# The low part of a converted weight group is subtracted one step later, and the conversions begin one step later in the first slot

## The chip, the cores and the metric

The kernel runs on one core of one Trainium2 chip. The metric is the device time of one execution in microseconds (us); lower is better. Time before: a median of 1327.45 us over three executions (1324.56 to 1330.62).

## What is computed

Linear attention over 8 x 8 heads of 576 tokens, then a mixture of eight experts of which each token takes one, then a feed-forward network with a leaky ReLU:

```python
h = np.maximum(x[mask] @ w1[e], 0.0)
out[mask] = gate_w[mask, None] * (h @ w2[e])      # 4608 tokens, 512 -> 1024 -> 512
...
h = x @ w_in                                       # 512 -> 2048
g = np.maximum(0.01 * h, h)
return g @ w_out                                   # 2048 -> 512
```

The weights `w_in` and `w_out` arrive as float64 words; the kernel turns them into float32 itself, by integer operations on their halves.

## The kernel before

Products of float32 are formed from halves: `split` (L508) lets ScalarE round a tile to a high part (L509, a CAST) and VectorE subtract it from the source, which leaves the low part (L510). TensorE then adds three products: high by high, low by high, high by low.

The experts' work is cut into slots of 512 tokens of one expert. Nine slots are always run (the first of them, slot 0, is in two functions, `slot0` and `slot0b`), and the rest stand under branches. A slot has two passes. In **pass 1** (`pass1`, L657) eight groups of 12 matmuls (L666) make the hidden rows; each group is followed by a ReLU on ScalarE (L668), which writes the high part, and by its low part on VectorE (L669). In **pass 2** (`pass2`, L672) four groups of 24 matmuls (L677) make the output rows; each is copied out by ScalarE (L683) and stored.

Beside them a slot prepares the next one, in an order that is written out by hand, every engine doing its instructions in that order:

- `wsplit` splits a quarter of an expert's weights, staged in a ring of five tiles `st` (L600): four for this slot's second product during pass 1, four for the next slot's first product during pass 2.
- `xload` gathers the next slot's tokens by GpSimd (L632), `xgate` scales the four gathered tiles on ScalarE (L641).
- `xprep(k)` turns a quarter of them by four transposes on TensorE into one of **two** buffers `tp` in PSUM (L652); ScalarE writes the high part (L654), VectorE the low part (L655), which frees the buffer. In slots 1 to 8 quarters 0 and 1 are turned in the middle of pass 2's second group, quarters 2 and 3 in the middle of its third; in `slot0b` in the middle of the third and the fourth.

Into slots 0 to 7 the conversion of `w_in` and `w_out` is woven. `conversions` is a generator: its first step loads the first of 16 groups into a tile `w` (L708, two DMAs of 512 KB, from ScalarE's queue; later groups are loaded from SP's), then each group takes four steps in `f64`. Step 1: two operations on VectorE (L724, L725), then `behind()`, the stores of the group before (L741, L742), and `ahead()`, the load of the next group. Step 2: L729, L730. Step 3: L732, L733. Step 4: four short operations (L737, `r`), the high part `rh` by ScalarE and the low part `rl` by VectorE.

`slot(s)` calls a step after pass 1's groups 1, 3, 5 and 7 (from slot 4 on also after group 6), after pass 2's groups 0, 1 and 2, and in the middle of group 3. `slot0b` calls five steps: after groups 0, 1 and 2, in the middle of group 3 and after it. So in slots 1, 2, 3 and 7 a group's step 4 falls after pass 1's last group, and step 1 of the next one after pass 2's group 0.

Of the kernel before, what the change touches and what calls it, by code (L numbers as in the profile page):

```python
# [9 lines left out]
F32 = mybir.dt.float32  # L10
# [4 lines left out]
ALU = mybir.AluOpType  # L15
# [492 lines left out]
def split(nc, hi, lo, src, eng=None):  # L508
    nc.scalar.copy(out=hi, in_=src)  # L509
    (eng or nc.vector).tensor_tensor(out=lo, in0=src, in1=hi.bitcast(F32), op=ALU.subtract)  # L510
# [33 lines left out]
def experts(pools, tc, cst, a, region, xd, dense, did, wops):  # L544
    nc = tc.nc
# [60 lines left out]
    def loads_to(n):  # L606
        while nload[0] < min(n, len(items)):
            wload(*items[nload[0]])
            nload[0] += 1

    def wsplit(s, which, c, eng=None, most=len(items)):
        n = 8 * s + 4 * (which - 1) + c
        loads_to(n + 1)
        t = stage.pop((s, which, c))
        if which == 1:
            split(nc, w1h[:, :, 256 * c:256 * c + 256], w1l[:, :, 256 * c:256 * c + 256], t.rearrange("p (k f) -> p k f", k=4), eng)
        else:
            split(nc, w2h[:, 2 * c:2 * c + 2], w2l[:, 2 * c:2 * c + 2], t.rearrange("p (k f) -> p k f", k=2), eng)
        loads_to(min(n + 1 + AHEAD, most))

    def idload(s):
        if s < NSLOT:
            nc.sync.dma_start(out=idts[s % 3].rearrange("p t c -> p (t c)"),
                              in_=region[bass.ds(reg(s, 1, NE * NT), SLOT), :].rearrange("(p t) c -> p (t c)", t=4))
# [11 lines left out]
    def xload(s):  # L636
        xids(s)
        xgather(s)
# [4 lines left out]
    def xgate(s):  # L643
        for t in range(4):
            xgate1(s, t)
# [3 lines left out]
    def xprep(k, wait=False):  # L649
        tp = ps2.tile([128, 4, 128], F32, tag="t", name="tp")  # L650
        for t in range(4):
            nc.tensor.transpose(out=tp[:, t], in_=xg[:, t, 128 * k:128 * k + 128], identity=ident)  # L652
        hi, lo = (x[:, k].rearrange("d (p t) -> d t p", t=4) for x in (xh, xl))
        nc.scalar.copy(out=hi, in_=tp)  # L654
        low = lambda: nc.vector.tensor_tensor(out=lo, in0=tp, in1=hi.bitcast(F32), op=ALU.subtract)  # L655
        if wait:
            xlow[k] = low  # L657
        else:
            low()
# [12 lines left out]
    def pass2(d, o, mid, rows):  # L672
        yp = ps.tile([128, SLOT], F32, tag="kv", name="yp")
        n = 0
        for f in range(8):
            for w, h in ((w2h, hh[:, f]), (w2l, hh[:, f]), (w2h, hl[f])):
                nc.tensor.matmul(yp[:, rows], lhsT=w[:, f, 128 * d:128 * d + 128], rhs=h[:, rows], start=(n == 0), stop=(n == 23))  # L677
                n += 1
            if f == 3:
                mid()  # L680
        y = ys[cnt[1] % 2]
        cnt[1] += 1
        nc.scalar.copy(out=y[:, rows], in_=yp[:, rows])  # L683
        nc.scalar.dma_start(out=dense[128 * d:128 * d + 128, bass.ds(o, rows.stop)], in_=y[:, rows])
# [26 lines left out]
    def f64(cv, name, i, w, ahead, behind):  # L711

        V = nc.vector
        if name == "win":
            dst = wops["win"][i % 4].rearrange("p s h k f -> h k p s f")[:, i // 4]
        else:
            dst = wops["wout"].rearrange("s p h k f -> h k p s f")[:, i]
        w2 = w.rearrange("p b f w -> p (b f) w")
        lo, hi = w2[:, :, 0], w2[:, :, 1]
        r = cv.tile([128, 8, 256], F32, tag="r", name="r")  # L720
        rh = cv.tile([128, 7, 256], F32R, tag="rh", name="rh")
        rl = cv.tile([128, 7, 256], F32R, tag="rl", name="rl")
        t = r[:, 0:4].rearrange("p b f -> p (b f)").bitcast(I32)
        V.tensor_scalar(out=t, in0=hi, scalar1=0x7FFFFFFF, scalar2=None, op0=ALU.bitwise_and)  # L724
        V.tensor_scalar(out=t.bitcast(F32), in0=t.bitcast(F32), scalar1=CLAMP_LO, scalar2=CLAMP_HI, op0=ALU.max, op1=ALU.min)  # L725
        behind()
        ahead()
        yield
        V.tensor_scalar(out=lo, in0=lo, scalar1=29, scalar2=0x40000000, op0=ALU.logical_shift_right, op1=ALU.bitwise_xor)  # L729
        V.tensor_scalar(out=t, in0=t, scalar1=4, scalar2=1, op0=ALU.logical_shift_left, op1=ALU.logical_shift_right)  # L730
        yield
        V.tensor_tensor(out=t, in0=t, in1=lo, op=ALU.bitwise_xor)  # L732
        V.scalar_tensor_tensor(out=t, in0=hi, scalar=-0x80000000, in1=t, op0=ALU.bitwise_and, op1=ALU.bitwise_or)  # L733
        yield
        for k, (x, y, op) in enumerate(((0, 2, ALU.add), (4, 1, ALU.subtract), (1, 0, ALU.subtract), (3, 5, ALU.subtract)) if name == "win"
                                       else ((0, 1, ALU.subtract), (2, 4, ALU.subtract), (2, 0, ALU.subtract), (3, 5, ALU.subtract))):
            V.tensor_tensor(out=r[:, 4 + k], in0=r[:, x], in1=r[:, y], op=op)  # L737
        split(nc, rh, rl, r[:, 1:8])

        def store():  # L740
            nc.sync.dma_start(out=dst[0], in_=rh.bitcast(F32))  # L741
            nc.sync.dma_start(out=dst[1], in_=rl.bitcast(F32))  # L742

        yield store

    def conversions(cv):
        todo = [(name, i) for name in ("win", "wout") for i in range(8)]
        w = {0: f64_load(cv, *todo[0], nc.scalar)}
        yield

        def ahead(n):
            if n < len(todo):
                w[n] = f64_load(cv, *todo[n])

        store = lambda: None
        for n, (name, i) in enumerate(todo):
            for r in f64(cv, name, i, w.pop(n), lambda: ahead(n + 1), store):
                store = r or store
                yield
        store()  # L760
# [33 lines left out]
    def slot0b(step):  # L794
        rows = slice(0, SLOT)
        xload(1)
        loads_to(8 + AHEAD)
        idload(2)
        for t in range(4):
            def mid():  # L800
                if t == 0:
                    wsplit(1, 1, 0)
                elif t == 1:
                    xgate(1)
                else:
                    xprep(2 * t - 4)
                    xprep(2 * t - 3)
                if t == 3:
                    step()
            pass2(t, 0, mid, rows)  # L810
            if t < 3:
                wsplit(1, 1, t + 1)
            step()

    def slot(s, step=lambda: None, mid2=lambda t: None, rows=slice(0, SLOT), end=NSLOT):
        if s + 1 < NSLOT:
# [33 lines left out]
    def rest(ctx, pre):  # L850
        wp = ctx.enter_context(tc.tile_pool(name="wp", bufs=1, reuse_waits="tile"))
        ys.extend(wp.tile([128, DM], F32, name=f"y{i}") for i in range(2))
        with ExitStack() as cctx:
            conv = conversions(cctx.enter_context(tc.tile_pool(name="cv", bufs=1, side="right", reuse_waits="tile")))
            step = lambda: next(conv, None)
            slot0b(step)
            for s in range(1, NSTATIC - 1):
                slot(s, step=step)
            for _ in conv:
                pass  # L860
# [455 lines left out]
```

## Time and profile before

| | |
|---|---|
| median of the runs | 1327.45 us (1324.56 to 1330.62) |
| the profiled execution's own time | 1331.54 us |
| its span, first to last instruction | 1329.7 us |
| TensorE busy | 1284.1 us, 97% |
| VectorE busy | 1044.5 us, 79% |
| ScalarE busy | 601.8 us, 45% |
| GpSimd busy | 348.3 us, 26% |
| mean granted TensorE clock | 0.991 |
| DMA | 274.69 MB, mean 207 GB/s |

The profile shows one execution. 1.9 us of its time lie outside the span. A share over the whole span says little here, since the program has four stages (attention to about 163 us, the experts' slots to 606 us, then the two products of the feed-forward network). What a change in the slots is worth is read there: from how long a slot's two passes take, and from what TensorE waits for.

### The profile page before, as it was taken

How to read it: one execution, taken by the hardware profiler on the slowest of the kernel's cores; microseconds unless marked ns; L12 is line 12 of the kernel's file. 1: busy time of each engine (PE TensorE's matmuls, PEld its weight loads, DVE VectorE, ACT ScalarE, POOL GpSimd, SP SyncE). 2: the span in 40 equal slices, each digit the busy share in tenths (PEclk: the TensorE clock that was granted, in tenths of full speed). 3: DMA queues.
4: the chain of work that ended last, by engine and by line, in shares of the span. 5: the costliest groups of instructions: out<-in, count | busy, mean ns of one | idle time of the engine just before them, and what ended most of it. 6: DMA issues, size and time to landing. Idle time of an engine off the chain costs nothing.

```text
span 1329.7 us, 21460 instructions
## 1 busy us (share of the span) xinstructions
PE 1284.1 (97%) x8161; PEld 1159.2 (87%) x8161; DVE 1044.5 (79%) x1375; ACT 601.8 (45%) x956; POOL 348.3 (26%) x283
## 2 busy tenths in 40 slices
PE   6999799999999999999999999999999999999998
PEld 6888677888888877899999999999978888888887
DVE  5789866788778878655888888888788888888886
ACT  4656435554555556452333233333244444444543
POOL 2227851011101110111433434433412221121121
PEclk9999899999999999999999999999999999999999
DMA  9876437879789887867833343333895354443430
GB/s 370 349 282 206 145 108 249 271 248 307 252 276 294 289 272 236 280 205 262 318 119 128 128 158 128 131 124 126 340 369 187 119 158 143 136 150 121 128 119 32
DMA packets 143088, 274.69 MB, mean 207 GB/s; under 512 B 17920, under 2 KB 67584, under 8 KB 142080
## 3 DMA queue, kind: packets, MB, share of 16 engines
q1 hardware_dynamic: 117936, 203.73, 45.5%
q10 hardware_dynamic: 17488, 48.48, 9.1%
q0 software_dynamic: 7552, 21.02, 4.5%
q8 instruction: 66, 1.08, 0.3%
q14 instruction: 46, 0.38, 0.1%
HBM read 176.87 MB, written 96.32 MB: 205 GB/s over the span
## 4 chain that ended last, share of the span: by engine, by line
PE 52%; issue 24%; POOL 6%; DMA 3%; DVE 3%; ACT 1%; another core or an unknown queue 1%; POOLq 0%; ACTq 0%; SPq 0%; DVEq 0%
PE hp L971 25%; PE hp L666 13%; PE yp L677 13%; POOL out L1156 4%; DMA wi<-wid 1%; PE tp L652 1%; DMA xg<-xd,idi 1%; POOL region L363 1%; DMA hd<-ht 1%; POOL q L227 0%; DVE xv L510 0%; POOL xg L632 0%; DVE xq L655 0%; ACT rh L509 0%
## 5 line engine op out<-in xcount | busy, mean ns | idle before, releaser
L971 PE MATMUL hp<-xh,wi 128*128 128x256 f32 x1152 | 211.4, 281 | 1.0 <-DMA wi<-wid 0.8
L666 PE MATMUL hp<-xq,xk 128*128 128x512 f32 (+1 forms) x640 | 189.7, 380 | 0.3 <-DVE xr L262 0.3
L971 PEld LDWEIGHTS hp<-xh,wi 128*128 128x128 f32 x1152 | 179.6, 189 | 1.3 <-ACT xh L509 1.0
L971 PE MATMUL hp<-x,wi 128*128 128x256 f32 x1296 | 161.5, 283 | 1.9 <-issue 1.8
L971 PE MATMUL hp<-xl,wi 128*128 128x256 f32 x576 | 161.8, 281 | 0.0
L971 PEld LDWEIGHTS hp<-x,wi 128*128 128x128 f32 x1296 | 157.9, 190 | 2.2 <-issue 2.2
L632 POOL DMA_INDIRECT xg<-xd,idi x44 | 54.8, 1245 | 356.4 <-ACT xq L668 228.1
L677 PE MATMUL yp<-xq,xk 128*128 128x512 f32 (+1 forms) x400 | 142.1, 385 | 0.8 <-DVE xq L669 0.8
L666 PEld LDWEIGHTS hp<-xq,xk 128*128 128x128 f32 x640 | 118.4, 189 | 23.3 <-DVE xr L262 0.8
L1156 POOL DMA_INDIRECT out<-yo,cf x36 | 59.3, 1647 | 291.7 <-DVE yo L1153 289.3
L1171 PE MATMUL yp<-wi,x 128*128 128x256 f32 x480 | 134.5, 280 | 1.2 <-DVE x L510 1.0
L1170 PE MATMUL yp<-wi,wi 128*128 128x512 f32 x384 | 134.8, 392 | 0.5 <-ACT wi L509 0.5
L510 DVE TENSOR_TENSOR xv<-st,xk 128x1024 fp32r<-128x1024 f32 x77 | 94.6, 1230 | 48.0 <-ACT xk L509 46.8
L677 PE MATMUL yp<-xq,xv 128*128 128x512 f32 (+1 forms) x320 | 122.0, 381 | 0.0
L666 PE MATMUL hp<-xq,xv 128*128 128x512 f32 (+1 forms) x320 | 121.3, 379 | 0.0
L985 DVE SCALAR_TENSOR_TENSOR ht<-ht 128x1024 f32<-128x1024 f32 (+1 forms) x73 | 112.5, 1550 | 1.9
L971 PEld LDWEIGHTS hp<-xl,wi 128*128 128x128 f32 x576 | 108.7, 189 | 0.0
L1018 POOL TENSOR_TENSOR s<-s,s 128x512 f32<-128x512 f32 x36 | 49.5, 1375 | 181.6 <-DVE s L1015 99.7
L1171 PEld LDWEIGHTS yp<-wi,x 128*128 128x128 f32 x480 | 90.1, 188 | 2.1 <-DVE x L510 2.1
L509 ACT CAST xk<-st 128x1024 fp32r<-128x1024 f32 x80 | 83.5, 1046 | 14.8 <-ACT y L683 8.3
L677 PEld LDWEIGHTS yp<-xq,xk 128*128 128x128 f32 x400 | 75.2, 190 | 14.9 <-DVE xq L669 1.2
L1170 PEld LDWEIGHTS yp<-wi,wi 128*128 128x128 f32 x384 | 72.1, 188 | 16.6 <-ACT wi L509 0.8
(227 smaller groups left out, 2804.9 us busy)
## 6 DMA issues: line engine op xcount, KB each, us to landing
st<-in_w SPq DMA_DIRECT2D x80, 512.0 KB
hd<-ht ACTq DMA_DIRECT2D x70, 512.0 KB
xt<-hd SPq DMA_DIRECT2D x18, 1024.0 KB
wi<-hd SPq DMA_DIRECT2D x18, 1024.0 KB
wi<-wid SPq DMA_DIRECT2D x28, 512.0 KB
v<-in_v SPq DMA_DIRECT2D x16, 650.0 KB
wi<-wod SPq DMA_DIRECT2D x5, 2048.0 KB
k<-in_k SPq DMA_DIRECT2D x16, 576.0 KB
```

The lines of the kernel that those rows point to most:

```text
L363: ins = nc.gpsimd.indirect_dma_start(out=region, out_offset=bass.IndirectOffsetOnAxis(ap=t["ix"][:, c:c + 1], axis=0), in_=t["tg"][:, c], ...
L509: nc.scalar.copy(out=hi, in_=src)
L510: (eng or nc.vector).tensor_tensor(out=lo, in0=src, in1=hi.bitcast(F32), op=ALU.subtract)
L632: nc.gpsimd.indirect_dma_start(out=xg[:, t], out_offset=None, in_=xd[0:n], in_offset=bass.IndirectOffsetOnAxis(ap=idis[s % 2][:, t:t + 1], ...
L666: nc.tensor.matmul(hp[:, rows], lhsT=w[:, k, 128 * f:128 * f + 128], rhs=x[:, k, rows], start=(n == 0), stop=(n == 11))
L677: nc.tensor.matmul(yp[:, rows], lhsT=w[:, f, 128 * d:128 * d + 128], rhs=h[:, rows], start=(n == 0), stop=(n == 23))
L971: self.nc.tensor.matmul(bank[:, g], lhsT=w[:, h, k, 128 * g:128 * g + 128], rhs=x[:, k], start=(n == 0), stop=(n == 5))
L985: V.scalar_tensor_tensor(out=c, in0=c, scalar=0.01, in1=c, op0=ALU.mult, op1=ALU.max)
L1018: G.tensor_tensor(out=s[6], in0=s[6], in1=s[5], op=ALU.add)
L1156: ins = nc.gpsimd.indirect_dma_start(out=out, out_offset=bass.IndirectOffsetOnAxis(ap=idi[s % 2][:, t:t + 1], axis=0), in_=yo[s % 2][:, t] ...
L1170: nc.tensor.matmul(bank, lhsT=oh[:, k], rhs=w[i][:, :, k], start=(fresh and k == 0), stop=False, skip_group_check=not fresh)
L1171: nc.tensor.matmul(bank[:, 1], lhsT=ol[:, k], rhs=w[i][:, 0, k], start=False, stop=(k == 7), skip_group_check=not fresh)
```

## The change

Four edits, in two parts.

The low part: `rl` is no longer computed in step 4, right behind ScalarE's cast to `rh`, but in the store function, just before the two stores are issued. `behind()`, which runs that function for the group before, moves from the end of step 1 to its start, ahead of L724 (L725 in the new numbering).

The steps of `slot0b`: none is taken after group 0; two, one behind the other, are taken after group 3. So the first load of the conversions and every step of the first group come one place later; from slot 1 on the steps lie as before.

```diff
         lo, hi = w2[:, :, 0], w2[:, :, 1]
+        behind()
         r = cv.tile([128, 8, 256], F32, tag="r", name="r")
...
         V.tensor_scalar(out=t.bitcast(F32), in0=t.bitcast(F32), scalar1=CLAMP_LO, scalar2=CLAMP_HI, op0=ALU.max, op1=ALU.min)
-        behind()
         ahead()
         yield
...
-        split(nc, rh, rl, r[:, 1:8])
+        nc.scalar.copy(out=rh, in_=r[:, 1:8])
 
         def store():
+            V.tensor_tensor(out=rl, in0=r[:, 1:8], in1=rh.bitcast(F32), op=ALU.subtract)
             nc.sync.dma_start(out=dst[0], in_=rh.bitcast(F32))
             nc.sync.dma_start(out=dst[1], in_=rl.bitcast(F32))
...
             pass2(t, 0, mid, rows)
             if t < 3:
                 wsplit(1, 1, t + 1)
-            step()
+            if t:
+                step()
+            if t == 3:
+                step()
```

VectorE's order from the last step of a group in slot 1 (after pass 1) to the two low parts of the gathered tokens in the middle of pass 2's second group; `xv` is the low part of a quarter of weights, `xq<-tp` that of a quarter of tokens:

```order
 L737 TENSOR_TENSOR r<-r 128x256 x4
-L510 TENSOR_TENSOR rl<-r,rh 128x1792
 L510 TENSOR_TENSOR xv<-st_110,xk 128x4x256
 L510 TENSOR_TENSOR xv<-st_111,xk 128x4x256
-L724 TENSOR_SCALAR r<-w 128x1024
-L725 TENSOR_SCALAR r<-r 128x1024
+L741 TENSOR_TENSOR rl<-r,rh 128x1792
+L725 TENSOR_SCALAR r<-w 128x1024
+L726 TENSOR_SCALAR r<-r 128x1024
 L655 TENSOR_TENSOR xq<-tp,xq 128x4x128 x2
```

The long subtraction goes from the far side of two weight splits to the near side: it now stands between them and the tokens' low parts, which free the `tp` buffers.

ScalarE's order in `slot0b`, from the copy of pass 2's group 0 to the casts of the first turned tokens, before:

```order
L683 COPY y_2208<-yp 128x512
L684 DMA dense<-y_2208 128x512
L509 CAST xk<-st_113 128x4x256
L708 DMA w<-in_win 128x2x512 x2
L641 ACTIVATE xg<-xg,idt_115 128x512 x4
L683 COPY y_2209<-yp 128x512
L684 DMA dense<-y_2209 128x512
L509 CAST xk<-st_109 128x4x256
L654 CAST xq<-tp 128x4x128 x2
```

And in the change, the same place:

```order
L683 COPY y_2208<-yp 128x512
L684 DMA dense<-y_2208 128x512
L509 CAST xk<-st_113 128x4x256
L641 ACTIVATE xg<-xg,idt_115 128x512 x4
L683 COPY y_2209<-yp 128x512
L684 DMA dense<-y_2209 128x512
L509 CAST xk<-st_109 128x4x256
L708 DMA w<-in_win 128x2x512 x2
L654 CAST xq<-tp 128x4x128 x2
```

The load of the first group goes from ahead of the four scalings of the gathered tokens to behind them. The load of the second group, on SP's queue, moves behind one more load of the ring (`st_109`) in the same way.

## Rows read from the trace of the kernel before

**Rows 1.** The page's part 1: busy us, share of the span, instructions of each engine.

```profile
PE 1284.1 (97%) x8161; PEld 1159.2 (87%) x8161; DVE 1044.5 (79%) x1375; ACT 601.8 (45%) x956; POOL 348.3 (26%) x283
```

**Rows 2.** Windows over pass 2 of slots 0 to 7: length, busy by engine, PEclk, DMA.

```profile
187.55:216.58 29.03, 25.85 (x113) 20.82 (x112) 14.06 (x18) 13.38 (x17) 5.12 (x4) 0.94 0.85 298
238.34:261.91 23.57, 23.57 (x113) 19.68 (x112) 17.57 (x21) 14.47 (x17) 0.00 (x0) 1.00 0.76 235
283.67:307.25 23.58, 23.58 (x114) 19.68 (x112) 17.57 (x21) 14.50 (x17) 0.00 (x0) 1.00 0.70 213
329.01:352.58 23.57, 23.57 (x113) 19.68 (x112) 17.56 (x21) 14.51 (x17) 0.00 (x0) 1.00 0.71 210
374.34:399.02 24.68, 23.87 (x113) 19.60 (x112) 19.37 (x25) 14.94 (x18) 0.00 (x0) 1.00 0.74 243
420.78:444.41 23.63, 23.63 (x114) 19.66 (x112) 20.55 (x23) 15.02 (x18) 0.00 (x0) 1.00 0.91 294
466.17:491.13 24.96, 24.01 (x114) 19.58 (x112) 20.79 (x25) 14.49 (x17) 0.00 (x0) 1.00 0.95 296
512.89:538.04 25.15, 24.30 (x113) 19.59 (x112) 19.82 (x23) 14.43 (x17) 0.00 (x0) 1.00 0.65 214
```

**Rows 3.** Groups by line and form: busy us, mean ns, idle before and releaser.

```profile
L510 DVE TENSOR_TENSOR rl<-r,rh 128x1792 fp32r<-128x1792 f32 x16 | 32.4, 2026 | 28.4 <-ACT rh L509 28.4
L509 ACT CAST rh<-r 128x1792 fp32r<-128x1792 f32 x16 | 27.2, 1698 | 53.1 <-DVE r L737 50.8 <-DMA idt<-region 2.3
```

**Rows 4.** Timeline of ScalarE and its queue in slot0b: start, us, instruction.

```profile
194.28 2.17 ACTq L708 DMA_DIRECT2D w<-in_win  x2
...
204.49 0.72 ACT L641 ACTIVATE xg<-xg,idt 128x512 f32<-128x512 f32 x1 [0.65 <-DMA xg<-xd,idi]
```

**Rows 5.** Timeline of TensorE in slot0b.

```profile
205.26 0.76 PE L652 MATMUL tp<-cf,xg 128*128 128x128 f32 x5 [1.04 <-ACT xg L641]
...
206.65 0.63 PE L677 MATMUL yp<-xv,xk 128*128 128x512 f32 x1
```

**Rows 6.** Timeline of VectorE, first group of the conversions and slot 1.

```profile
209.18 0.69 DVE L724 TENSOR_SCALAR r<-w 128x1024 int32<-128x1024 int32 x1 [0.76 <-DMA w<-in_win]
...
222.72 2.03 DVE L510 TENSOR_TENSOR rl<-r,rh 128x1792 fp32r<-128x1792 f32 x1 [1.83 <-ACT rh L509]
...
239.17 0.69 DVE L669 SCALAR_TENSOR_TENSOR xq<-hp,xq 128x512 fp32r<-128x512 f32 x1 [0.53 <-ACT xq L668]
239.78 1.54 DVE L737 TENSOR_TENSOR r<-r 128x256 f32<-128x256 f32 x4
```

**Rows 7.** Timeline of VectorE in slot 2, pass 2.

```profile
288.43 2.02 DVE L510 TENSOR_TENSOR rl<-r,rh 128x1792 fp32r<-128x1792 f32 x1 [1.77 <-ACT rh L509]
...
293.78 1.22 DVE L510 TENSOR_TENSOR xv<-st,xk 128x1024 fp32r<-128x1024 f32 x1 [0.71 <-ACT xk L509]
294.92 0.69 DVE L724 TENSOR_SCALAR r<-w 128x1024 int32<-128x1024 int32 x1
...
296.25 2.08 DVE L655 TENSOR_TENSOR xq<-tp,xq 128x512 fp32r<-128x512 f32 x2
```

**Rows 8.** Timeline of TensorE in slot 2, turning quarters 2 and 3.

```profile
298.19 1.03 PE L652 MATMUL tp<-cf,xg 128*128 128x128 f32 x8
```

**Rows 9.** Timeline of TensorE in slots 4, 6 and 7, and the branch at the slots' end.

```profile
380.53 0.73 PE L677 MATMUL yp<-xq,xk 128*128 128x512 f32 x2 [0.81 <-DVE xq L669]
...
481.42 0.66 PE L652 MATMUL tp<-cf,xg 128*128 128x128 f32 x4 [0.59 <-DVE xq L655]
...
528.38 0.65 PE L652 MATMUL tp<-cf,xg 128*128 128x128 f32 x4 [0.24 <-DVE xq L655]
...
608.37 3.89 PE L971 MATMUL hp<-x,wi 128*128 128x256 f32 x18 [1.80 <-issue]
```

**Rows 10.** Timeline of VectorE in slot 5, the last low part of pass 1.

```profile
425.10 0.68 DVE L669 SCALAR_TENSOR_TENSOR xq<-hp,xq 128x512 fp32r<-128x512 f32 x1
```

**Rows 11.** A window behind the branch: PEclk is the column after the counts.

```profile
608.70:612.10 3.40, 3.40 (x19) 3.40 (x18) 1.73 (x4) 1.97 (x4) 0.00 (x0) 0.50 0.52 157
```

## The prediction

> **What bounds the kernel now.** I read the page first: TensorE is busy 97% of the span [rows 1], so only what TensorE waits for can be won, and the change touches nothing outside the experts' slots. Then the windows over the second pass of each slot [rows 2]. The reader is to see the length: 23.57 us where nothing is in the way (slots 1, 2, 3), 29.03 in slot 0, 24.68 in slot 4, 23.63 in slot 5, 24.96 in slot 6, 25.15 in slot 7. The excess is 5.46, 1.11, 0.06, 1.39 and 1.58 us, 9.6 us in all, and that is the most this change can win.
>
> Then the groups by line [rows 3]: VectorE waits 28.4 us for ScalarE's cast to `rh`, 16 times, about 1.8 us each, and the subtraction behind it takes 2.03. That is the wait which the change removes. VectorE isn't the bound, so its 28.4 us count only where TensorE waits for VectorE. Last, the timelines of the places where TensorE stands still: in slot 0 for the scaled tokens [rows 5], which ScalarE can't scale before the gather has landed [rows 4]; in slots 4, 6 and 7 for a low part [rows 9].
>
> **The change, part by part.** All sums are against the slots' lengths in this one execution (1331.54 us; the median of the runs, 1327.45, is 4.1 lower, and I add the difference to the median).
>
> *The load in slot 0.* The first load of the conversions is issued at 194.28 [rows 4], while the gather is on its way, and the second follows from SP's queue: 2.1 MB which, at the 298 GB/s of this window [rows 2], are 7.0 us of the DMA engines' time. Both now go behind the scalings. Of the 5.46 us of excess about 1.7 are the clock (granted 0.94 of 29.03 us [rows 2]; a matmul then takes 0.63 us [rows 5]), so the stall itself is some 3.7. If only half of the 7.0 us reaches the gather, it lands 3.5 sooner, and 0.2 of the stall stays. I take **-5.2**; the ends are -5.5 and, with a quarter of it, -1.8 (the clock then still falls).
>
> What the moved load now sits in front of: on ScalarE's queue its two DMAs take 2.17 us [rows 4] ahead of the first casts of turned tokens, which TensorE needs only a whole group of 24 matmuls later; cost nothing. On VectorE the first operation of group 0 still comes at about 209.2, as it did [rows 6], since the same weight split stands before it, now together with two tokens' low parts. For that the load must have landed. It is now issued behind four scalings of 0.72 [rows 4], a copy and a cast, some 7.4 us later than before, at about 201.7, and shares the engines with 0.26 MB of output and 0.52 MB of ring load: 1.84 MB at 298 GB/s are 6.2 us, so 207.9, in time. The other end is the time it took before, 194.28 to 209.1 [rows 4, 6], 14.8 us: it would be at 216.5, 7.3 us late. I take the first, since the queues that made those 14.8 us are what the change empties.
>
> By the Trainium skill's "DMA: Bandwidth & Descriptors" (Anatomy of one DMA) a transfer pays about 2 us beside its bytes, most of it for the receipt of the last write; by that page's figure (an estimate) the load would be there at 209.9, 0.7 us late, and the sum 0.7 higher. No row here isolates that cost.
>
> *Slot 1.* TensorE now comes 5.2 us sooner, VectorE doesn't. Between its operations at 209.18 and 239.78 [rows 6] lie 30.6 us, of them 1.83 + 0.53 waits, so 28.2 of work. Ahead of 209.2 now stand two low parts of tokens, 2.08, and one weight split, 1.14 [rows 7]: 25.0 remain, `rl` among them. A wait of 2.3 comes in: slot 1's first low part needs a ReLU that ScalarE does only after the cast (1.70 [rows 3] and some 0.6). So the four short operations of step 4 start at 209.2 + 27.3 = 236.5. TensorE begins pass 2 at 238.34 - 5.2 = 233.1: they come 3.4 us into it, against 1.44 before, 2.0 later (2.2 if the gain is 5.4). Cast, scalings, weight splits and low parts follow in one chain on ScalarE and VectorE, so TensorE is held up by about that much, on top of what slots 2 and 3 pay: **+3.8**, between 1.7 and 4.5.
>
> *Slots 2 and 3 (the same place).* Before, `rl` ran where VectorE had time: it idled behind it. Now it stands directly before L724, L725 and the two low parts of tokens. These began at 296.25 [rows 7], took 1.04 each, and the first was done 0.9 us before TensorE wanted its buffer at 298.19 [rows 8]. VectorE's order is fixed, and the weight split at 293.78 waits for ScalarE [rows 7], which follows TensorE; so nothing before it can move up. `rl` adds 1.94 (2.03 less the overlap seen between neighbours): first low part at 299.24, TensorE 1.1 late; four transposes take 0.4 to 0.5, second low part at 300.3, 0.6 late. **+1.7 each, +3.4.** The bounds are 1.0 (one wait of 1.94 less 0.9) and 1.94.
>
> *Slot 4.* The low part that TensorE awaits (0.81 [rows 9]) stood behind `rl`, and comes about 3.8 - 2.3 = 1.5 us sooner: **-1.1**, all of it. *Slot 6.* The awaited low parts stood behind `rl` too; they are then held by ScalarE's own cast alone, and of 1.39 I leave 0.4: **-1.0**. *Slot 5.* Here `rl` moves from before pass 1's group 6 to after it, between two low parts. The last one [rows 10] had no slack (0.06 us of excess); before, it had a wait of 1.8 in front, now one of 2.3 (cast and ReLU): **+0.5**. *Slot 7.* As slots 2 and 3, but TensorE already waited for these low parts (0.24 [rows 9]), so the whole 1.94 shows: **+1.9**.
>
> *At nothing:* the two stores leave up to 6 us later, and SP's queue waits there for `rl`, with a group's load and ring loads behind it. Their readers come four steps (a slot's half) later; without that room each late load would stop VectorE as in [rows 6] (0.76). GpSimd's gathers get their indices some 3.8 us sooner in slots 1 to 4; nobody waits for that.
>
> Sum: -5.2 + 3.8 + 3.4 - 1.1 + 0.5 - 1.0 + 1.9 = **+2.3**.
>
> *The clock.* In slots 1 and 7 TensorE would now stand still for about 2 us and again for 0.6. A stop of 1.80 us at the slots' end [rows 9] was followed by a clock of half speed (0.50 [rows 11]), and so were three of about 1 us close together in slot 0 [rows 2, 5]; stops of 0.6 in slot 6 and 0.8 in slot 4 were not (1.00 [rows 2]). The new ones are nearest the first. A fall costs 1.7 us (slot 0, above). I take one fall for the two places, **+1.7**, with 0 and 3.4 as ends. In all +4.0: 1335.5 for the profiled execution, and **1331.5** on the median.
>
> **The rivals.**
> 1. *VectorE's won time reaches TensorE* (the other side). The 28.4 us make VectorE so early that slots 1, 2, 3 and 7 pay nothing and all stalls go: 9.6 us off, 1317.9. For it: 28.4 us are a lot, and the stalls of slots 4, 6 and 7 are all VectorE's. It decides at slot 2: with 1.94 us or more of slack between the low part and TensorE. Against it: that slack is 0.9. Chance 0.05.
> 2. *The give-back is partial*: slots 2, 3 and 7 pay, slot 1 only its 1.7, no clock falls: 2.3 - 2.1 = +0.2, 1327.7. Chance 0.2.
> 3. *The load is late.* The first group's load lands as slowly as before; VectorE starts up to 7.3 us late with two low parts of tokens queued behind it, and TensorE waits for those in slot 1: up to 1338.8, on the middle 1335. Chance 0.12.
> 4. *The clock falls in both places or in more* (slots 2 and 3 stand still for 1.7 us in two pieces): 1333.2 and, for a third fall, 1334.9. Chance 0.15.
> 5. *The change doesn't remove the wait*, because the next step follows too closely. The nearest two steps are a whole group of pass 1 apart, longer than the cast's 1.70; under 0.02, and counted with the second.
>
> **How the numbers follow.** My forecast (+1.5 to +5.5) has 0.48, the rivals 0.05, 0.2, 0.12 and 0.15. Half a per cent, about what a measurement of this kernel can tell from no change, is 6.6 us: under 1320.8 or over 1334.1. Faster: the first rival less its milder half, 0.04. Slower: three quarters of the third and half of the fourth, with some of the forecast's upper end and the runs' own spread of 3.2 us above the median: 0.2. Within: 0.76. The range goes from the second rival less that the median may move by 2 (1325.7) to the third at most of its price: 1325.5 to 1337.5.
>
> **What would show it.** In the changed profile: VectorE's wait before `rl` is gone (28.4 to near 0); slot 0's second pass is 23.6 to 24.1 us long and its scalings don't wait for the gather; slot 1's is 27 to 28, slots 2 and 3 about 25.3 with TensorE waiting at L652 for L655; slot 4 is 23.6, slot 5 24.1, slot 6 24.0, slot 7 27. Slots 2 and 3 at 23.57 would prove the main step wrong; a wait for `w` before the first L725 would speak for the third rival, a PEclk under 1.00 in slots 1 or 7 for the clock's term.

## The result, and the profile after

The change made the kernel slower: a median of 1337.15 us over 11 runs (1332.25 to 1341.62) against 1326.24 for the kernel before (11 runs, 1323.47 to 1330.89). The ratio is 1.0068 with an interval of [1.0051, 1.0085], so between 6.8 and 11.3 us, 9.0 on the middle (the two medians lie 10.9 apart). That is outside the half per cent within which I had put it with a chance of 0.76, and above the +1.5 to +5.5 of the forecast. The time itself lies just inside the upper edge of the range, by luck: that edge was put there for the third rival, the late load, and something else filled it.

The profiled execution of the change took 1337.22 us (span 1335.4, mean granted clock 0.993), 5.7 more than that of before (1331.54, 1329.7, 0.991).

The wait ahead of `rl` goes, as the change intends. The page's first part and the groups by line, to be read beside [rows 1] and [rows 3]:

```profile
PE 1283.0 (96%) x8161; PEld 1156.0 (87%) x8161; DVE 1044.3 (78%) x1375; ACT 599.9 (45%) x956; POOL 347.8 (26%) x283
```

```profile
L741 DVE TENSOR_TENSOR rl<-r,rh 128x1792 fp32r<-128x1792 f32 x16 | 32.3, 2018 | 3.5 <-ACT rh L738 3.5
L738 ACT CAST rh<-r 128x1792 fp32r<-128x1792 f32 x16 | 27.1, 1696 | 59.0 <-DVE r L737 53.9 <-DMA idt<-region 5.1
```

The work is the same to 0.2 us on VectorE, and its idle time ahead of `rl` has gone from 28.4 us to 3.5. But VectorE as a whole has won nothing: span less busy time is 285.2 us before and 291.1 after. The 24.9 us of waiting moved to other operations. The low parts of the experts' weights and of the tokens, first before, then after:

```profile
L510 DVE TENSOR_TENSOR xv<-st,xk 128x1024 fp32r<-128x1024 f32 x77 | 94.6, 1230 | 48.0 <-ACT xk L509 46.8 <-issue 1.1
L655 DVE TENSOR_TENSOR xq<-tp,xq 128x512 fp32r<-128x512 f32 x40 | 41.4, 1078 | 2.4 <-ACT xq L654 2.4
```

```profile
L510 DVE TENSOR_TENSOR xv<-st,xk 128x1024 fp32r<-128x1024 f32 x77 | 94.6, 1229 | 63.6 <-ACT xk L509 63.6
L655 DVE TENSOR_TENSOR xq<-tp,xq 128x512 fp32r<-128x512 f32 x40 | 41.1, 1072 | 7.9 <-ACT xq L654 7.9
```

Before these two VectorE waits 15.6 and 5.5 us longer than it did, in both for ScalarE.

Where the loss is, the windows over pass 2 of slots 0 to 7 tell (length, then busy time by engine, and after the counts the granted clock, the DMA share and GB/s):

```profile
185.77:210.33 24.56, 24.04 (x113) 19.69 (x112) 9.84 (x13) 13.10 (x16) 4.59 (x4) 1.00 0.89 302
232.26:262.12 29.86, 26.42 (x113) 20.76 (x112) 20.89 (x24) 14.37 (x17) 0.00 (x0) 0.94 0.83 255
283.88:309.27 25.39, 24.02 (x113) 19.59 (x112) 17.53 (x21) 14.53 (x17) 0.00 (x0) 1.00 0.75 237
331.03:356.40 25.37, 24.00 (x114) 19.58 (x112) 17.54 (x21) 14.53 (x17) 0.00 (x0) 1.00 0.76 230
378.16:401.73 23.57, 23.57 (x113) 19.67 (x112) 19.44 (x25) 14.82 (x18) 0.00 (x0) 1.00 0.76 254
423.49:448.02 24.53, 23.91 (x113) 19.60 (x112) 19.51 (x23) 14.96 (x18) 0.00 (x0) 1.00 0.85 274
469.78:493.72 23.94, 23.78 (x113) 19.66 (x112) 20.18 (x24) 14.26 (x17) 0.00 (x0) 1.00 0.88 279
515.49:542.70 27.21, 24.35 (x113) 19.59 (x112) 19.83 (x23) 14.37 (x17) 0.00 (x0) 1.00 0.69 231
```

Against [rows 2]: slot 0 is shorter by 4.47 us, and slots 4 and 6 by 1.11 and 1.02; slot 1 is longer by 6.29, slots 2 and 3 by 1.81 and 1.80, slot 5 by 0.90, slot 7 by 2.06. The sum is +6.3, somewhat more than the 5.7 us between the two profiled executions.

How it comes about is seen in slot 2. VectorE's timeline there (start, us, instruction; in brackets the wait before it), to be laid beside [rows 7]:

```profile
293.97 1.23 DVE L510 TENSOR_TENSOR xv<-st,xk 128x1024 fp32r<-128x1024 f32 x1 [0.72 <-ACT xk L509]
295.11 2.02 DVE L741 TENSOR_TENSOR rl<-r,rh 128x1792 fp32r<-128x1792 f32 x1
297.17 0.69 DVE L725 TENSOR_SCALAR r<-w 128x1024 int32<-128x1024 int32 x1
297.89 0.70 DVE L726 TENSOR_SCALAR r<-r 128x1024 f32<-128x1024 f32 x1
298.50 2.02 DVE L655 TENSOR_TENSOR xq<-tp,xq 128x512 fp32r<-128x512 f32 x2
```

The weight split comes as it did (293.97 against 293.78); `rl` now stands between it and the rest of the chain, and the tokens' low parts start at 298.50 instead of 296.25. TensorE's timeline shows who pays, in slots 1, 2 and 7 in order of time; before, all eight transposes of slot 2 ran without a stop [rows 8]:

```profile
250.89 0.66 PE L652 MATMUL tp<-cf,xg 128*128 128x128 f32 x4 [2.27 <-DVE xq L655]
251.86 0.66 PE L652 MATMUL tp<-cf,xg 128*128 128x128 f32 x4 [0.32 <-DVE xq L655]
...
299.61 0.66 PE L652 MATMUL tp<-cf,xg 128*128 128x128 f32 x4 [1.05 <-DVE xq L655]
300.58 0.66 PE L652 MATMUL tp<-cf,xg 128*128 128x128 f32 x4 [0.32 <-DVE xq L655]
...
533.06 0.66 PE L652 MATMUL tp<-cf,xg 128*128 128x128 f32 x4 [2.26 <-DVE xq L655]
534.03 0.66 PE L652 MATMUL tp<-cf,xg 128*128 128x128 f32 x4 [0.32 <-DVE xq L655]
```

In slot 2 it is 1.05 + 0.32 us of waiting; the rest of the 1.81 is mostly that transposes in two broken pieces of 0.66 take longer than eight in a row, 1.03. In slot 7, where TensorE waited 0.24 [rows 9] and then 0.33 before, it is 2.26 and 0.32. Over the whole span, the waits of TensorE put together by what ended them (us, times, longest):

```profile
PE tp L652 <- DVE xq L655: 8.1, 9, 2.3
PE tp L652 <- ACT xg L641: 1.6, 6, 0.3
```

The first of these groups had 1.5 us in the kernel before, the second 3.5: the wait for the scaled tokens has been traded for a longer one for the tokens' low parts.

Slot 1's stop of 2.27 us has a second price. A window that begins behind it:

```profile
252.50:255.80 3.30, 3.30 (x10) 2.55 (x9) 3.30 (x5) 1.20 (x2) 0.00 (x0) 0.50 1.08 304
```

The granted clock is 0.50, the lower of the two levels, and ten matmuls fill the 3.30 us. No such window is in slot 7, after a stop as long.

### The profile page after: what moved, and what is told of

Read it like the earlier page. It is cut to its first block, busy times and chain, and to the rows that moved or that the text cites. A ratio compares the mean times of both kernels' runs of the same rounds, so it can differ in the third digit from the quotient of the medians.

```text
span 1335.4 us, 21459 instructions
## 1 busy us (share of the span) xinstructions
PE 1283.0 (96%) x8161; PEld 1156.0 (87%) x8161; DVE 1044.3 (78%) x1375; ACT 599.9 (45%) x956; POOL 347.8 (26%) x283
## 4 chain that ended last, share of the span: by engine, by line
PE 47%; issue 24%; DVE 6%; POOL 5%; DMA 4%; ACT 3%; ACTq 0%; POOLq 0%; SPq 0%; DVEq 0%
PE hp L975 24%; PE hp L666 12%; PE yp L677 9%; POOL out L1160 4%; DMA wi<-wid 2%; DVE rl L741 1%; DVE xq L655 1%; ACT xk L509 1%; ACT xg L641 1%; PE tp L652 1%; DMA st<-in_w 1%; DVE r L737 1%; DMA xg<-xd,idi 1%; DMA hd<-ht 1%; DMA w<-in_win 1%
## 5 line engine op out<-in xcount | busy, mean ns | idle before, releaser
L668 ACT ACTIVATE xq<-hp 128x512 fp32r<-128x512 f32 (+1 forms) x80 | 46.0, 577 | 90.7 <-PE hp L666 83.8
```

The costliest lines, as they stand in the source:

```text
L668: nc.scalar.activation(out=hh[:, f, rows], in_=hp[:, rows], func=AF.Relu)
```

## The experiments

All lengths are of second passes (us), slots 0 to 8; "sum" goes from the start of slot 0's second pass to the end of slot 8's. The kernels before and after were profiled more than once, since the first pair of traces left the size of one term open, and 10 is the kernel of 5 again.

| kernel | 0 | 1 | 2 | 3 | 4 | 5 | 6 | 7 | 8 | sum |
|---|---|---|---|---|---|---|---|---|---|---|
| before | 29.03 | 23.57 | 23.57 | 23.57 | 24.68 | 23.63 | 24.96 | 25.15 | 23.57 | 395.8 |
| before again (6) | 25.34 | 23.55 | 23.55 | 23.55 | 24.67 | 23.58 | 24.91 | 25.14 | 23.57 | 391.9 |
| before again (8) | 26.39 | 23.57 | 23.57 | 23.57 | 24.67 | 23.61 | 24.97 | 25.16 | 23.57 | 393.2 |
| after | 24.56 | 29.86 | 25.39 | 25.37 | 23.57 | 24.53 | 23.94 | 27.22 | 23.57 | 402.3 |
| after again (7) | 25.24 | 29.39 | 25.37 | 25.39 | 23.57 | 24.51 | 23.96 | 27.22 | 23.57 | 402.3 |
| 1 steps only | 24.91 | 24.64 | 23.57 | 23.57 | 24.69 | 23.57 | 24.95 | 25.14 | 23.57 | 393.7 |
| 2 low part only | 27.03 | 27.73 | 25.39 | 25.37 | 23.57 | 24.49 | 23.95 | 27.22 | 23.57 | 402.4 |
| 3 two groups | 24.45 | 24.63 | 23.57 | 23.57 | 23.57 | 23.57 | 23.95 | 25.14 | 23.57 | 391.0 |
| 4 short operations later | 24.59 | 26.41 | 23.97 | 24.01 | 23.89 | 23.57 | 23.95 | 25.84 | 23.57 | 393.9 |
| 5 both | 24.83 | 23.65 | 23.57 | 23.57 | 23.86 | 23.57 | 23.95 | 24.23 | 23.57 | 389.6 |
| 9 both, early steps | 24.34 | 23.57 | 23.57 | 23.57 | 23.87 | 23.57 | 23.95 | 24.23 | 23.57 | 388.3 |
| 10 as 5 | 25.76 | 23.66 | 23.57 | 23.57 | 23.87 | 23.57 | 23.95 | 24.23 | 23.57 | 390.5 |

**1. The later steps alone.** The kernel before, with only `slot0b`'s steps changed:

```diff
-            step()
+            if t:
+                step()
+            if t == 3:
+                step()
```

> The kernel before with the later steps of slot0b alone; the low part is back behind the cast. Theory (the low part's new place makes TensorE wait for the two tp buffers, the later steps only help): slot 0's second pass about 24.5 us, slots 2, 3 and 7 back at 23.6, 23.6 and 25.2, slot 4 24.7, slot 6 25.0; slot 1 about 24.6, since VectorE starts its first group no earlier while TensorE comes sooner. 3 to 5 us faster than before. Rival (the later first load is what costs, because the first group is late): slot 1 stays near 29 and the time is 3 us or more slower than before.

Measured: 1326.58 us against 1326.8, ratio 0.9996 [0.9981, 1.0012]. The windows of slots 0 and 1:

```profile
187.93:212.83 24.90, 23.82 (x113) 19.67 (x112) 9.95 (x13) 13.21 (x16) 4.12 (x4) 1.00 0.89 297
235.61:260.25 24.64, 24.11 (x113) 19.58 (x112) 19.34 (x23) 14.37 (x17) 0.00 (x0) 1.00 0.82 250
```

Slot 0 is short, but slot 1 gives back 1.07 us in its second pass and 1.02 in its first (22.78 against 21.76, with a wait of 0.72 for VectorE's low part). So the times show no gain from the later steps, where 3 to 5 us were expected: that expectation had booked all of slot 0's first 29.03 us.

**2. The late low part alone.** The change, with `slot0b`'s steps as before:

```diff
-            if t:
-                step()
-            if t == 3:
-                step()
+            step()
```

> The kernel before with the later low part alone; slot0b takes its steps as before. Theory: slot 0 stays at 29, slots 1, 2 and 3 at 25.4 to 26.2, slot 4 23.6, slot 5 24.5, slot 6 24.0, slot 7 27.2: 6 to 8 us slower than before, so about as slow as or slower than both parts together less the clock's share. Rival (the first load's delay is the cost): within 2 us of before. Second rival (SP's queue, which now waits for the low part, delays loads): slots 2 and 3 long because ScalarE or VectorE waits for DMA there, not because TensorE waits for the tokens' low part.

Measured: 1335.76 us over 6 runs against 1326.8, ratio 1.0070 [1.0049, 1.0091]: the whole loss, somewhat more than the 6 to 8 us expected. Windows of slots 0, 1 and 2:

```profile
185.25:212.28 27.03, 24.45 (x113) 19.61 (x112) 11.97 (x16) 13.18 (x16) 4.97 (x4) 1.00 0.88 313
234.04:261.77 27.73, 25.63 (x113) 20.86 (x112) 18.75 (x22) 14.51 (x17) 0.00 (x0) 0.94 0.82 261
283.53:308.92 25.39, 24.01 (x113) 19.59 (x112) 17.51 (x21) 14.52 (x17) 0.00 (x0) 1.00 0.74 235
```

and TensorE's first transposes in slot 2 wait as in the change:

```profile
299.25 0.66 PE L652 MATMUL tp<-cf,xg 128*128 128x128 f32 x4 [1.05 <-DVE xq L655]
```

Slots 2 to 7 are those of the change to 0.04 us, so the steps of slot 0 have no part in them. Slot 1 pays here too, and its clock falls here too (0.94); it pays 2.1 us less than in the change, but more than the 25.4 to 26.2 expected, which had no fall in them. Slot 0 is 2.5 longer than in the change, and not the 29 expected.

**3. The low part late in two groups only.** Groups 7 and 12, whose subtraction stood in the way in slots 4 and 6, keep the late place; the other fourteen subtract right behind the cast. The late steps stay.

```diff
         nc.scalar.copy(out=rh, in_=r[:, 1:8])
+        later = (name, i) in (("win", 7), ("wout", 4))
-        def store():
+        def low():
             V.tensor_tensor(out=rl, in0=r[:, 1:8], in1=rh.bitcast(F32), op=ALU.subtract)
+        if not later:
+            low()
+        def store():
+            if later:
+                low()
```

> The changed kernel, with the low part deferred for groups 7 and 12 alone (the ones whose step 4 falls before something that TensorE awaits in slots 4 and 6); the other fourteen subtract right behind the cast. Theory: slot 0 24.5, slot 1 24.6, slots 2, 3 and 5 23.6, slot 4 23.6, slot 6 24.0, slot 7 25.2: about 2 us faster than the later steps alone, 5 to 7 faster than before, and the fastest of these kernels. Rival (deferring costs wherever it is done): no faster than the later steps alone.

Measured: 1324.85 us against 1326.8, ratio 0.9986 [0.997, 1.0002]. Windows of slots 2, 4 and 6:

```profile
280.32:303.90 23.58, 23.58 (x114) 19.68 (x112) 17.57 (x21) 14.49 (x17) 0.00 (x0) 1.00 0.70 212
...
370.99:394.56 23.57, 23.57 (x113) 19.69 (x112) 19.47 (x25) 14.83 (x18) 0.00 (x0) 1.00 0.74 255
...
461.66:485.60 23.94, 23.77 (x113) 19.68 (x112) 19.27 (x23) 14.23 (x17) 0.00 (x0) 1.00 0.80 248
```

Slots 4 and 6 keep all that the change won there, and slots 2, 3, 5 and 7 pay nothing. By the slots, gains and losses of the change thus belong to different groups of weights and can be had apart. The time is 1.9 us shorter, within the noise, and not the 5 to 7 expected: again slot 0 had been booked at its first length.

**4. The short operations out of the way.** The change, with L725 and L726 (0.69 + 0.70 us) one step later, so that `rl` alone stands before the tokens' low parts. If a stall is made by the amount of VectorE's work in that place, it shrinks by what is taken out; if the late stores on SP's queue made it, nothing changes.

```diff
-        V.tensor_scalar(out=t, in0=hi, scalar1=0x7FFFFFFF, scalar2=None, op0=ALU.bitwise_and)
-        V.tensor_scalar(out=t.bitcast(F32), in0=t.bitcast(F32), scalar1=CLAMP_LO, scalar2=CLAMP_HI, op0=ALU.max, op1=ALU.min)
         ahead()
         yield
+        V.tensor_scalar(out=t, in0=hi, scalar1=0x7FFFFFFF, scalar2=None, op0=ALU.bitwise_and)
+        V.tensor_scalar(out=t.bitcast(F32), in0=t.bitcast(F32), scalar1=CLAMP_LO, scalar2=CLAMP_HI, op0=ALU.max, op1=ALU.min)
```

> The changed kernel, with the two operations of a group's step 1 moved to the head of its step 2, so that only the low part (1.94 us) stands before the tokens' low parts and no longer 1.94 + 1.33. Theory (what counts is how much VectorE work stands in that place): slots 2 and 3 24.1 instead of 25.4, slot 7 26.0 instead of 27.2, slot 1 about 1.3 shorter: 5 to 6 us faster than the changed kernel. Rival (the stores and loads behind the low part on SP's queue cost the time; they stay where they are): slots 2, 3 and 7 unchanged.

Measured: 1328.4 us against 1326.8, ratio 1.0008 [0.9994, 1.0021]. Windows of slots 1, 2 and 7:

```profile
233.30:259.71 26.41, 24.65 (x113) 19.61 (x112) 20.34 (x24) 14.34 (x17) 0.00 (x0) 1.00 0.83 254
281.48:305.45 23.97, 23.80 (x114) 19.67 (x112) 17.44 (x21) 14.50 (x17) 0.00 (x0) 1.00 0.73 226
...
509.67:535.51 25.84, 24.42 (x114) 19.60 (x112) 19.79 (x23) 14.35 (x17) 0.00 (x0) 1.00 0.74 245
```

and slot 2's timeline, VectorE and TensorE:

```profile
292.70 2.02 DVE L741 TENSOR_TENSOR rl<-r,rh 128x1792 fp32r<-128x1792 f32 x1
...
294.64 2.07 DVE L655 TENSOR_TENSOR xq<-tp,xq 128x512 fp32r<-128x512 f32 x2
...
296.76 0.66 PE L652 MATMUL tp<-cf,xg 128*128 128x128 f32 x4 [0.17 <-DVE xq L655]
```

With 1.4 us less ahead of the low parts, slots 2 and 3 are 1.42 and 1.36 us shorter, slot 7 is 1.38 shorter, and in slot 1, which is 3.45 shorter, the clock stays at 1.00 (slot 4 loses 0.32 of its gain, slot 5's loss is gone). What was left is a wait of 0.17. `rl` and its stores are as late as in the change, so the queue of the stores did not make these 1.4 us: it is the work in front of the low parts, us for us. Against the kernel before, the loss of 9.0 us is down to 1.1, about 8 us less, where 5 to 6 less were expected; the expectation had counted neither slot 1's clock nor slot 5.

**5 and 10. Both remedies.** Experiments 3 and 4 in one kernel (no further edit):

> The kernel with the low part deferred for groups 7 and 12 alone, and with step 1's two operations at the head of step 2. Theory: the second pass of slot 7 goes from 25.14 to about 24.4 and that of slot 1 from 24.63 to about 23.8, slot 4 may lose 0.3 of its gain, the others stay at 23.6 to 24.0: 1 to 1.5 us faster than the two groups alone, and about 3.5 us (0.25%) faster than before. Rival (moving the two operations gains nothing once the low part is out of the way): the same time as the two groups alone.

> The kernel with two groups deferred, step 1's operations moved and the later steps, again on this chip beside the one above: slots as in its first profile to 0.2 us, 2 to 4 us faster than before. By the theory the one above is within 2 us of it; by its rival 3 us slower.

Measured: 1329.22 us against 1331.12, ratio 0.9982 [0.9964, 0.9999]; in the second measurement (10) 1323.97 against 1325.81, 0.9989 [0.9974, 1.0003]. Windows of slots 1 and 7 in the first of them:

```profile
239.65:263.30 23.65, 23.65 (x114) 19.67 (x113) 19.01 (x23) 14.29 (x17) 0.00 (x0) 1.00 0.82 254
...
512.39:536.62 24.23, 23.95 (x113) 19.69 (x112) 19.62 (x23) 14.30 (x17) 0.00 (x0) 1.00 0.68 224
```

Slot 7 is now 0.9 us better than before the change: the two short operations have left the front of its low parts, and the waits of 0.24 and 0.33 are gone. Slots 1 and 7 come out as expected, the time does not: the gain is 1.5 to 2.4 us, where about 3.5 and 2 to 4 were expected, and below what a measurement of this kernel surely tells from none. Nor does slot 0 repeat to the 0.2 us expected: 24.83, then 25.76.

**6, 7 and 8. More traces of before and after.** The sums of the first pair differ by 6.4 us, while the timed runs differ by 9.0. These three ran on one chip, no edit: before (6), after (7), before (8).

> The kernel before once more, for a second profile. Theory (the first profile of before was of an execution with a long stall in slot 0 and a fall of the clock behind it, so that the gain was read too large): slot 0's second pass is 26 to 27.5 us instead of 29.03, the other slots as before to 0.1. Rival (29.03 is what this kernel always takes there): 29.0 again.

> The changed kernel once more, for a second profile. Theory: the slots' second passes repeat to 0.1 us (25.4, 25.4, 23.6, 24.5, 23.9, 27.2 for slots 2 to 7) unless the clock falls at another place: slot 7 is then 1.7 longer, or slot 1 1.7 shorter. Rival (the stalls of the first profile were of that execution): slots 2, 3 and 7 differ by 0.5 or more without a fall of the clock.

> The kernel before a third time. As for the second profile: slot 0's second pass at 26 to 27.5 us by the theory, 29.0 by its rival; all other slots as in the first profile.

Measured, one time each: 1334.41, 1342.48 and 1334.09 us. Slot 0's second pass in the two traces of before, first (6), then (8):

```profile
193.27:218.61 25.34, 23.97 (x113) 19.66 (x112) 11.97 (x16) 13.19 (x16) 4.04 (x4) 1.00 0.91 324
```

```profile
191.82:218.21 26.39, 24.45 (x114) 19.59 (x113) 11.94 (x16) 13.17 (x16) 4.39 (x4) 1.00 0.90 318
```

and slots 0, 1 and 7 of after (7):

```profile
191.66:216.91 25.25, 24.02 (x114) 19.69 (x113) 10.65 (x13) 13.21 (x16) 4.59 (x4) 1.00 0.88 299
238.66:268.06 29.40, 26.27 (x114) 20.76 (x112) 20.43 (x24) 14.37 (x17) 0.00 (x0) 0.94 0.81 260
...
521.42:548.64 27.22, 24.36 (x113) 19.59 (x112) 19.83 (x23) 14.39 (x17) 0.00 (x0) 1.00 0.68 231
```

Every other slot repeats to 0.1 us, slot 1 with its fall to 0.5; slot 0 of the kernel before does not: 29.03 with a clock of 0.94 and 298 GB/s in the first trace [rows 2], 25.34 (below the 26 to 27.5 expected) and 26.39 with a clock of 1.00 and 324 and 318 GB/s in these. On this chip the sums of before and after differ by 9.8 us on the mean, the three times by 8.2.

These lengths say nothing of the rest of the program. Outside the slots of the table, where no edit changes anything, the span less the sum is 933.9 us in the first trace of before, 940.6 and 939.0 in (6) and (8), and between 928.7 and 940.6 in all twelve traces. The times of two single executions can thus differ by more than this change costs without any cause in the slots.

**9. Both remedies, without the later steps.** Experiment 5 with `slot0b`'s steps as before; the edit to the steps is that of experiment 2.

> The kernel with the low part deferred for two groups and step 1's operations moved, but with slot0b's steps as before (the first one after group 0). Theory (the later steps of slot0b gain nothing on the whole: what slot 0 wins, slot 1 gives back, since VectorE is late there either way): slot 0's second pass 25 to 29 and slot 1's first and second 21.8 and 23.6, the other slots as with the later steps; 1 to 3 us faster than before, within 2 us of the kernel with the later steps. Rival (the later steps carry that kernel's gain): no faster than before, slot 0 and slot 1 together 3 us longer than with the later steps.

Measured: 1323.24 us against 1325.81, ratio 0.9989 [0.9978, 1.0], the same as experiment 10 beside it, and a gain of 1.5 us for the 1 to 3 expected. Windows of slots 0 and 1:

```profile
186.99:211.33 24.34, 23.79 (x113) 19.66 (x112) 11.21 (x15) 13.16 (x16) 4.04 (x4) 1.00 0.98 347
233.09:256.67 23.58, 23.58 (x114) 19.67 (x112) 18.98 (x22) 14.29 (x17) 0.00 (x0) 1.00 0.81 250
```

The shortest slot 0 of all kernels has the early load, and slot 1 is free of any wait. By the slots this is the version to take: the low part late in two groups, the two short operations one step later, and nothing changed in `slot0b`. By its time it can't be told from experiment 10, and hardly from the kernel before.

## Why the prediction was right about the places and wrong about the size

*VectorE's wait, and that it doesn't reach TensorE: right.* The 28.4 us went to 3.5, VectorE waited elsewhere instead, and slots 1, 2, 3 and 7 paid. The first rival (all stalls go) falls with slot 2, where it was to be decided. So does the fifth: the wait ahead of `rl` was removed.

*Slots 2 and 3: right.* +1.81 and +1.80 for +1.7, with 1.05 + 0.32 us of waiting for 1.1 and 0.6; the broken transposes, which the forecast didn't count, made up for the second wait. Experiment 4 shows the cause. *Slot 7: right,* +2.06 for +1.9. *Slots 4 and 6: right,* -1.11 and -1.02 for -1.1 and -1.0, and experiment 3 shows which groups bring them. *Slot 5: too small,* +0.90 for +0.5.

*Slot 1 and the clock: right in kind, small by 0.8.* 6.29 us against 3.8 + 1.7. The clock fell once in the two places, as taken, and in slot 1 in all three traces of a kernel with the late low parts as they stand in the change (after, after again, experiment 2). So the second rival (no fall) and the fourth (two or three) fall. Experiment 2 splits the term: with `slot0b`'s steps as before, the late low part holds up slot 1 by 4.2 us, the fall included; the other 2.1 come with the later steps, for 2.0 in the forecast.

*The load: right, in time enough.* VectorE and ScalarE around slot 0, from their two timelines:

```profile
208.94 0.69 DVE L725 TENSOR_SCALAR r<-w 128x1024 int32<-128x1024 int32 x1 [1.26 <-DMA w<-in_win]
```

```profile
199.21 1.33 ACT L641 ACTIVATE xg<-xg,idt 128x512 f32<-128x512 f32 x2 [1.92 <-DMA xg<-xd,idi]
201.50 0.95 ACTq L708 DMA_DIRECT2D w<-in_win  x2
```

Slot 0's second pass begins 1.78 us earlier in this execution than in the first one (185.77 for 187.55), so the forecast's points in time have to be moved by as much. The load was issued at 201.50, 15.7 us into the pass, for a forecast of 14.2 (201.7): the forecast that the scalings wouldn't wait for the gather was wrong. ScalarE still waited 1.92 us, and slot 0 kept 1.0 us of excess. The load was there at 208.94 or just before, 7.4 us after its issue, for a forecast of 6.2. VectorE waited 1.26 us for it, which is the sign that I had named for the third rival, but a sixth of what that rival had. Slot 1's first pass is 0.17 us longer than before, 21.93 against 21.76; in after again (7) it is not. The other end, 14.8 us, was far off, and the third rival falls. By the Trainium skill's "DMA: Bandwidth & Descriptors" (Anatomy of one DMA) the estimate had been 2 us more than the bytes, 8.2; the page gives that figure for transfers that GpSimd issues, and ScalarE issues this one. The trace lies midway between the sum of the bytes and that estimate, and decides for neither.

*Slot 0: the step that failed.* The term "-5.2", with ends -5.5 and -1.8. Against that one execution it measured -4.47. But what it removes was mostly not there in other executions: its 5.46 us of excess, 1.7 of them a fall of the clock, were 1.77 and 2.82 us in the two later traces. The slot 0 of kernels with the early load measured 29.03, 25.34, 26.39 and 27.03 (before three times, experiment 2), 26.95 on the mean; with the late load 24.56, 25.24, 24.91, 24.45, 24.59, 24.83 and 25.76, 24.91 on the mean. So the term is about -2.0, near the end that I had called the milder. Experiment 9, early and 24.34, shows that even this isn't sure: the two ranges overlap.

Nor was the gather all of it. In the third trace of before (8), TensorE waited 0.68 us in slot 0 for the scaled tokens, and more for VectorE, whose low parts stood behind a wait for the early load and the two short operations:

```profile
211.54 0.69 DVE L724 TENSOR_SCALAR r<-w 128x1024 int32<-128x1024 int32 x1 [1.57 <-DMA w<-in_win]
...
213.99 0.66 PE L652 MATMUL tp<-cf,xg 128*128 128x128 f32 x4 [0.94 <-DVE xq L655]
214.96 0.66 PE L652 MATMUL tp<-cf,xg 128*128 128x128 f32 x4 [0.32 <-DVE xq L655]
```

As in slot 2 of the change, operations of the conversion stand in front of low parts that TensorE awaits. Experiment 9 has the two operations one step later and no such wait in slot 0; that this is why its slot 0 is the shortest is not shown by one trace.

With this one term put at -2.0, the measured ones give -2.0 + 6.29 + 0.17 + 3.61 - 1.11 + 0.90 - 1.02 + 2.06 = +8.9, where the timed runs have 9.0, between 6.8 and 11.3; with slot 0 as uncertain as above, so close a fit is partly chance. In my sum, 3.2 of the 4.9 us that were missing are slot 0's, 0.8 slot 1's, and the rest slots 5, 2, 3 and 7 and slot 1's first pass with 0.2 to 0.4 each.

The step was also inconsistent in itself: I moved the total to the median by subtracting 4.1 us, because the profiled execution (1331.54 us) was longer than the median, and still booked in full, as a gain on the median, a stall that may have been part of those 4.1. With the milder end, +3.4 on the sum, the forecast would have been 1334.9. But that the 4.1 us lay in slot 0 is not shown: the later traces of before (6 and 8) are of executions 3 us longer than that chip's median, 1331.12, and have the short slot 0; their slot 0 begins its second pass at 193.27 and 191.82 us instead of 187.55. The length of an execution doesn't tell which of its stalls will repeat; a second trace does.

What stays open: how often the kernel before has the long stall in slot 0 (three traces of it can't tell), and why slot 0's load meets the gather harder in some executions.

## What to carry to other kernels

The price of a moved instruction is set by what stands right behind it on its engine in the new place: `rl` was free where VectorE waited anyway, and cost up to its whole length in front of the low parts that TensorE waited for. That the wait ahead of `rl` fell by 25 us said nothing: VectorE's idle time as a whole did not fall, since it then waited for ScalarE at the next operations. Defer work only for those groups whose own place is in somebody's way (here two of sixteen), and not by a rule for all. A stall that depends on a transfer's landing or on the clock is booked as a gain only after a second trace shows it too.

## What the runs showed of the hardware that was not expected

- Two stops of the same length had different consequences: 2.27 and 0.32 us in slot 1 were followed by a granted clock of 0.50, and 2.26 and 0.32 us in slot 7 left it at 1.00; after again (7) shows the same by its windows, 0.94 and 1.00. In experiment 2 even a shorter stop in slot 1 went with a fall (0.94 in its window), so the length of the stop alone doesn't decide:

```profile
250.48 0.66 PE L652 MATMUL tp<-cf,xg 128*128 128x128 f32 x4 [1.77 <-DVE xq L655]
```

- The load of the first group took 14.8 us from issue to its reader in the early place and 7.4 in the late one, at a rate of the whole core of about 300 GB/s in both windows. Other traces agree: 13.0 and 13.6 us early (8, experiment 2; in (6) it was there within 11.9), 6.8 and 7.3 late (7, experiment 1). The issue of its two DMAs on ScalarE's queue took 2.17 us in the first trace of before [rows 4], but 1.07 and 0.92 in the same place in (6) and (8), and 0.95 in the late place: the 2.17 are of that execution.
- With the same code, the second pass of slot 0 took between 25.34 and 29.03 us, while the second passes of slots 2 and 3 repeated to 0.03 us.
